# A third expert's first layer in seven half products, and two experts interleaved on four PSUM banks

## The chip, the cores and the metric

The kernel runs on one core of a Trainium2 chip. The metric is the device time of one execution in microseconds (us), the median of several runs. Engines are named as in the profile: PE is TensorE's matmul stream, PEld its weight loads, DVE is VectorE, ACT is ScalarE, POOL is GpSimd, SP is SyncE, which here only issues DMAs.

## What is computed

A windowed and causal attention over 4 batches, 8 heads and 768 positions gives a matrix x of 3072 tokens by 512 features. A dense mixture of four experts follows, in which every token goes through every expert:

```python
p = domain_probs / (domain_probs.sum(-1, keepdims=True) + 1e-09)
out = np.zeros((N, D), dtype=np.float32)          # N = 3072, D = 512
for e in range(E):                                # E = 4, F = 1024
    h = np.maximum(x @ w1[e], 0.0)
    out += p[:, e:e + 1] * (h @ w2[e])
```

The change touches only the product `x @ w1[e]` (the first layer) of the last tokens.

## The kernel before, in words

The order of every engine's instructions is written by hand: the kernel is one Python program that issues instructions in the order in which each engine will run them. Operands in SBUF are float16, sums in PSUM are float32. PSUM has eight banks here: four called pA, two called pV (attention's value products), two called pO.

The 24 tiles of 128 tokens are done as follows: three tiles and then one tile by plain matmuls (`plain_steps`), and then ten pairs of tiles, 256 tokens each (`pair_steps`, L1171), the pairs beginning at tiles 4, 6, ... 22. Attention for later tokens is mixed in between these steps; its last matmul in the trace is at 288.5 us, so that the last three pairs (tiles 18, 20 and 22) have the engines to themselves.

A pair has two layers.

**Layer 1** is `x @ w1[e]` for each expert, with the tokens already scaled by the expert's probability (`scale_inputs`, L1124, one DVE multiply of 128x1024 numbers, or two of 128x512 where the pair straddles a chunk of 384 tokens). A plain expert (`plain_layer1`, L1173) is four steps of eight matmuls of 256 columns, each step ended by one ACT relu that writes hidden values to the tile hA. An expert "by seven half products" (`winograd_layer1`, L1201) is Winograd's form of Strassen's scheme: the 512x1024 weights and the 512x256 tokens are cut into 2x2 blocks, and seven products of blocks take the place of eight. Each product is eight matmuls of 128 columns. The steps of one such expert are:

1. product on bank x, then an ACT copy of x to SBUF (`keep`, L1218)
2. product on a pA bank z, then a DVE add with saturation at zero (`add`, L1225) that writes one quarter of the hidden values
3. product added onto bank x, then a second ACT copy
4. product on bank y, a third ACT copy, and a small DVE subtraction on the tokens
5. product added onto x, then a DVE add
6. product added onto y, then a DVE add
7. product added onto x, then an ACT relu (L1258)

A product that adds onto a bank has to wait until the copy or add that reads that bank is done. Sums of token blocks (`scaled_sums`, L1147, three small DVE instructions) and sums of weight blocks (`first_weight_sums`, L1006, four DVE instructions of 128x1024, done once for an expert) feed the products. Before the last three pairs one expert (number 3) goes by half products; in the last three pairs experts 3 and 2 do (`EW`), and experts 0 and 1 are plain. Expert 3 has bank x = the first of the two pO banks taken for the pair and y = the second; expert 2 has them the other way round (L1265).

The order of steps in the last three pairs is the list at L1290, where a is expert 3, b expert 2, n the plain experts 0 and then 1. After each group of steps an extra operation may follow:

```python
((a, a, n), None), ((a, a, n), load_probs), ((a, a, n), None), ((n,), scaled_sums(EW[1])),
((a, b, n), None), ((b, b, n), first_sum(0)), ((b, b, n), first_sum(EW[0])),
((b, n, b), (first_sum(1), first_sum(EW[1])))
```

**Layer 2** (from L1307) is again seven products, of 16 matmuls of 256 columns each, over the hidden values of all four experts. It takes two new pO tiles, x and y. Its first product goes to x (L1363), its second to y, its seventh to x, read by the ACT copy at L1418. Beside it DVE makes the next pair's scaled tokens: expert 1 (L1370), expert 3, expert 0, the token sums of expert 3 and, as the last of them, expert 2 (L1394).

The weights of experts 0 and 1 lie in SBUF with pairs of columns interleaved (`w1_tile`, L344), so that a weight load of these reads with a step of two.

Of the kernel before, what the change touches and what calls it, by code (L numbers as in the profile page):

```python
# [11 lines left out]
FP32 = mybir.dt.float32  # L12
FP16 = mybir.dt.float16
AF = mybir.ActivationFunctionType
ALU = mybir.AluOpType
# [4 lines left out]
def kernel(  # L20
# [34 lines left out]
    P = 128  # L55
    B, H, S, D = q.shape
    E, DM, F = moe_w1.shape
# [5 lines left out]
    DMP = DM // P  # L63
# [19 lines left out]
    WT = 7  # L83
# [259 lines left out]

    def w1_tile(e, ct, ft):  # L344

        x = w1sb[:, e * DMP + ct, :]
        if in_pairs(e):
            x = x[:, ft // 2 * 2 * P : (ft // 2 + 1) * 2 * P]
            return x.rearrange("p (x j) -> p j x", j=2)[:, ft % 2, :]
        return x[:, ft * P : (ft + 1) * P]  # L350
# [202 lines left out]
    def mm_ns(cols):  # L553
        return cols / 2.4 + 2.5
# [434 lines left out]
    def minus(out, a, b):  # L989
        nc.vector.tensor_tensor(out=out, in0=a, in1=b, op=ALU.subtract)  # L990
# [15 lines left out]
    def first_weight_sums(e):  # L1006

        return [
            lambda: minus(t1[e, 0], w1_part(e, 0, 1), w1_part(e, 0, 0)),
            lambda: minus(t1[e, 1], w1_part(e, 1, 1), t1[e, 0]),  # L1010
            lambda: minus(t1[e, 2], w1_part(e, 1, 0), t1[e, 1]),
            lambda: minus(w1_part(e, 0, 1), w1_part(e, 1, 1), w1_part(e, 0, 1)),
        ]

    def room_for_more_sums():
# [6 lines left out]
        x = att.tile([P, DMP * PC], FP16, name="xs1", tag="q16", bufs=1)  # L1022
        own_room[EW[1]] = x.rearrange("p (c x) -> p c x", c=DMP)

    own_room = {}

    def last_weight_sum(e):
# [68 lines left out]
    PC = PT * P  # L1096
# [42 lines left out]
    def x_part(e, i, j):  # L1139
        return scaled(e)[:, j * KH : (j + 1) * KH, i * P : (i + 1) * P]  # L1140

    def x_sum(n):

        n0 = WT * NSH * P + n * KH * P
        return kSf[:, n0 : n0 + KH * P].rearrange("p (c x) -> p c x", c=KH)

    def scaled_sums(e):  # L1147

        nc.vector.tensor_tensor(
            out=x_sum(0), in0=x_part(e, 1, 0), in1=x_part(e, 1, 1), op=ALU.add  # L1150
        )
        minus(x_sum(1), x_sum(0), x_part(e, 0, 0))
        minus(x_part(e, 1, 0), x_part(e, 0, 0), x_part(e, 1, 0))

    def first_sum(e, n=1):
# [11 lines left out]

    def two(nt0):
        return nt0 >= pairs[-LAST]

    def pair_steps(nt0, nxt):  # L1171

        def plain_layer1(e):  # L1173
            xs = scaled(e)
            for f0 in range(0, FTP, 2):
                ps = bank()
                for f in range(2):
                    for ct in range(DMP):
                        nc.tensor.matmul(  # L1179
                            out=ps[:, f * PC : (f + 1) * PC],  # L1180
                            lhsT=w1_tile(e, ct, f0 + f),
                            rhs=xs[:, ct, :],
                            start=(ct == 0),
                            stop=(ct == DMP - 1),
                        )
                b0 = 2 * (f0 // HT)
                k0 = e * HT + f0 % HT
                nc.scalar.activation(  # L1188
                    out=blocks[:, b0 : b0 + 2, k0 : k0 + 2, :].rearrange(
                        "p t f x -> p f t x"  # L1190
                    ),
                    in_=ps.rearrange("p (f t x) -> p f t x", f=2, t=2),
                    func=AF.Relu,
                )
                yield 2 * DMP * mm_ns(PC), 0.5
# [2 lines left out]
        kept = [s1[:, (n % 2) * HT * P : (n % 2 + 1) * HT * P] for n in range(3)]  # L1198
        banks = [pO.tile([P, DM], FP32, name="pO", bufs=2) for _ in range(2)]

        def winograd_layer1(e, x, y):  # L1201

            ns = HT * KH * mm_ns(P)

            def product(ps, w, a, first):
                for f in range(HT):
                    for ct in range(KH):
                        nc.tensor.matmul(  # L1208
                            out=ps[:, f * P : (f + 1) * P],
                            lhsT=w[:, ct, f * P : (f + 1) * P],  # L1210
                            rhs=a[:, ct, :],
                            start=(first and f == 0 and ct == 0),
                            stop=(ct == KH - 1),
                            skip_group_check=True,
                        )

            def keep(n, ps):
                nc.scalar.copy(out=kept[n], in_=ps)  # L1218

            def block(n):  # L1220
                return blocks[:, n, e * HT : (e + 1) * HT, :]

            def add(n, ps, b):

                nc.vector._custom_dve(  # L1225
                    TENSOR_ADD_SAT,
                    out=block(b),
                    in0=ps.rearrange("p (f x) -> p f x", f=HT),
                    in1=kept[n].rearrange("p (f x) -> p f x", f=HT),
                    s0=LARGEST,  # L1230
                    s1=0.0,
                )

            def t(n):
                return t1[e, n]

            product(x, w1_part(e, 0, 0), x_part(e, 0, 0), True)
            keep(0, x)
            yield ns, 0.5
            z = bank()  # L1240
            product(z, w1_part(e, 1, 0), x_part(e, 0, 1), True)
            add(0, z, 0)
            yield ns, 0.5
            product(x, t(1), x_sum(1), False)
            keep(1, x)
            yield ns, 0.5
            product(y, t(0), x_sum(0), True)
            keep(2, y)
            minus(x_part(e, 0, 1), x_part(e, 0, 1), x_sum(1))
            yield ns, 0.5  # L1250
            product(x, w1_part(e, 0, 1), x_part(e, 1, 0), False)
            add(2, x, 3)
            yield ns, 0.5
            product(y, w1_part(e, 1, 1), x_part(e, 0, 1), False)
            add(1, y, 2)
            yield ns, 0.5
            product(x, t(2), x_part(e, 1, 1), False)
            nc.scalar.activation(  # L1258
                out=block(1), in_=x.rearrange("p (f x) -> p f x", f=HT), func=AF.Relu
            )  # L1260
            yield ns, 0.5

        a, b = (winograd_layer1(e, *y) for e, y in zip(EW, (banks, banks[::-1])))  # L1265

        more, last_more = [], None
        if nt0 == pairs[-LAST - 2]:
            room_for_more_sums()
            more = first_weight_sums(EW[1])  # L1270
        elif nt0 == pairs[-LAST - 1]:
            last_more = first_weight_sums(EW[1])[3]
        if not two(nt0):
            n = itertools.chain(*(plain_layer1(e) for e in range(E - 1)))
            order = (
                ((n,), lambda: scale_inputs(nt0, 1)),
                ((n,), more[0] if more else None),
                ((n, a), lambda: last_weight_sum(E - 1) if nt0 == pair0 else None),
                ((n, a), None),
                ((n, a), lambda: scale_inputs(nt0, 2)),  # L1280
                ((n, a), lambda: load_probs(nxt)),
                ((n, a), more[1] if more else None),
                ((n, a), more[2] if more else None),
                ((n, a), lambda: first_sum(0, 2)),
                ((n,), None),
                ((n, n), lambda: first_sum(2, 2)),
                ((), lambda: scale_inputs(nxt, 1) if two(nxt) else None),
            )
        else:
            n = itertools.chain(plain_layer1(0), plain_layer1(1))  # L1290
            order = (
                ((a, a, n), None),
                ((a, a, n), lambda: load_probs(nxt) if nxt else None),
                ((a, a, n), None),
                ((n,), lambda: scaled_sums(EW[1])),
                ((a, b, n), None),
                ((b, b, n), lambda: first_sum(0)),
                ((b, b, n), lambda: first_sum(EW[0])),
                ((b, n, b), lambda: (first_sum(1), first_sum(EW[1]))),
            )  # L1300
# [12 lines left out]
        def product(ps, a, b, first, middle=None):  # L1313
            for k in range(KT):
                nc.tensor.matmul(  # L1315
                    out=ps,
                    lhsT=a[:, k, :],
                    rhs=b(k),
                    start=(first and k == 0),
                    stop=(k == KT - 1),  # L1320
                    skip_group_check=not first,
                )
                if k == KT // 2 - 1:
                    if middle is not None:
                        middle()
                    yield KT // 2 * mm_ns(HN), PSHARE
# [4 lines left out]
        def t(n):  # L1331
            return lambda kt: tsb[:, n, kt, :]
# [26 lines left out]

        last = nxt is None  # L1360
        ahead = nxt and two(nxt)
        half = KT // 2 * mm_ns(HN), PSHARE
        yield from product(x, A11, b(0, 0), True)  # L1363
        keep(0, x)
# [207 lines left out]
```

## Time and profile before

| | |
|---|---|
| median of 6 runs | 377.98 us (377.49 to 378.89) |
| profiled execution | 377.49 us, span of instructions 375.7 us |
| PE busy in the span | 368.2 us (98%) |
| DVE / ACT / POOL busy | 271.4 / 228.0 / 112.5 us |
| mean granted TensorE clock | 0.998 |
| pair 20, layer 1 and layer 2 on PE | 321.32 to 334.56 and 334.56 to 346.78 us |
| pair 22, layer 1 | 346.78 to 360.02 us |

In the profile each row of a timeline is a run of like instructions: start, time until the last one ended, engine and line, operation, what it writes and reads, the count, and, where the engine stood idle before it, for how long and who ended that. Matmuls are pipelined, so the duration of a row of matmuls has the last one's latency in it; the pace of PE is read from the distance between starts.

### The profile page before, as it was taken

To read this page: it belongs to the slowest core of one execution; us is meant where nothing else is said; L and a number is where in the kernel's file an instruction comes from. 1 tells how busy PE (TensorE), PEld (TensorE's weight loads), DVE (VectorE), ACT (ScalarE), POOL (GpSimd) and SP (SyncE) were. 2 spreads that over 40 slices of the span, in tenths; PEclk is the share of its full clock that TensorE was granted. 3 is DMA by queue.
4 is the path that set the end of the run, shared out by engine and by line. 5 is a ranking of instruction groups with operands and counts; after the bars stand their busy time and mean duration, and the time that the engine had idled before them with its cause. 6 is when DMAs were issued, how large, how long until landed. Compare 5 with 4: busy or idle time off the path is not lost.

```text
span 375.7 us, 10100 instructions
## 1 busy us (share of the span) xinstructions
PE 368.2 (98%) x4128; PEld 310.9 (83%) x4128; DVE 271.4 (72%) x581; ACT 228.0 (61%) x475; POOL 112.5 (30%) x155
## 2 busy tenths in 40 slices
PE   8899999999999999999999999999999999999996
PEld 4754466668998988999989898998899998999995
DVE  7774868697787669868668858967768758559461
ACT  3863479547785785765776855784777361551630
POOL 8924673854057039115501650320000000000000
PEclk9999999999999999999999999999999999999999
DMA  9999999999599499978905991951220300300001
GB/s 167 151 202 208 194 185 193 172 177 145 97 116 156 87 98 128 161 106 70 192 5 66 172 154 27 130 117 11 72 68 3 114 2 0 114 2 23 36 2 57
DMA packets 123747, 39.24 MB, mean 104 GB/s; under 512 B 113728, under 2 KB 116356, under 8 KB 123700
## 3 DMA queue, kind: packets, MB, share of 16 engines
q0 software_dynamic: 85824, 19.01, 60.5%
q1 hardware_dynamic: 36276, 19.18, 22.4%
q8 instruction: 32, 0.52, 0.6%
q10 hardware_dynamic: 1600, 0.39, 0.5%
q14 instruction: 15, 0.12, 0.1%
HBM read 44.89 MB, written 6.34 MB: 136 GB/s over the span
## 4 chain that ended last, share of the span: by engine, by line
PE 95%; DVE 2%; ACT 2%; issue 0%; ACTq 0%
PE pO L1315 31%; PE pA L1179 25%; PE pO L1208 9%; PE pA L1050 7%; PE pO L1071 7%; PE pA L676 5%; PE pV L732 2%; PE pV L804 2%; PE pA L1208 2%; PE pO L446 1%; PE pA L574 1%; ACT es L694 1%; DVE xs L1135 1%; PE pA L1405 0%; ACT rc L822 0%; DVE xT L827 0%
## 5 line engine op out<-in xcount | busy, mean ns | idle before, releaser
L1315 PEld LDWEIGHTS <-hA 128*128 128x128 f16 x1104 | 104.8, 98 | 12.3
L1179 PE MATMUL pA<-xs,w1sb 128*128 128x256 f16 x864 | 109.3, 272 | 0.0
L1179 PEld LDWEIGHTS <-w1sb 128*128 128x128 f16 x864 | 80.7, 98 | 8.5
L1188 ACT ACTIVATE hA<-pA 128x512 f16<-128x512 f32 x108 | 64.4, 598 | 35.2 <-PE pA L1179 32.9
L1315 PE MATMUL pO<-w2sb,hA 128*128 128x256 f16 x640 | 76.7, 272 | 0.0
L694 ACT ACTIVATE es<-pA 128x384 f16<-128x384 f32 (+2 forms) x122 | 59.2, 511 | 26.6 <-PE pA L676 22.9
L306 POOL DMA_DIRECT2D vS<-in_v_dram x30 | 29.6, 986 | 110.0 <-PE pV L804 108.2
L1315 PE MATMUL pO<-tsb,hA 128*128 128x256 f16 x464 | 56.7, 272 | 0.0
L1135 DVE TENSOR_TENSOR xs<-xT,pB 128x1024 f16<-128x1024 f16 (+1 forms) x52 | 49.5, 970 | 1.3 <-DMA xT<-x_pair 1.2
L990 DVE TENSOR_TENSOR hA<-hA 128x1024 f16<-128x1024 f16 x60 | 39.6, 684 | 0.4
L1063 ACT ACTIVATE hA<-pA 128x384 f16<-128x384 f32 (+1 forms) x64 | 22.2, 385 | 19.5 <-PE pA L1050 19.3
L1050 PE MATMUL pA<-xT,w1sb 128*128 128x384 f16 (+1 forms) x256 | 31.1, 273 | 0.7 <-DMA w1sb<-in_moe_w_dram 0.3
L1071 PE MATMUL pO<-w2sb,hA 128*128 128x512 f16 x128 | 30.7, 379 | 0.0
L1335 ACT COPY s<-pO 128x256 f32<-128x256 f32 x31 | 11.6, 373 | 27.7 <-PE pO L1315 21.9
L827 DVE TENSOR_TENSOR xT<-pV,rc 64x384 f16<-64x384 f32 x37 | 20.5, 555 | 10.5 <-ACT rc L832 8.1
L1050 PEld LDWEIGHTS <-w1sb 128*128 128x128 f16 x256 | 19.4, 98 | 9.8 <-issue 1.5
L1208 PEld LDWEIGHTS <-w1sb 128*128 128x128 f16 x416 | 26.3, 98 | 1.1 <-issue 0.2
L1225 DVE CUSTOM_DVE_ANT_0 hA<-pO,s 128x512 f16<-128x512 f32 x26 | 17.7, 689 | 12.5 <-PE pO L1208 8.8
L822 ACT ACTIVATE rc<-pV,eps 64x384 f32<-64x384 f32 x37 | 21.3, 576 | 6.5 <-PE pV L804 5.9
L698 DVE TENSOR_TENSOR es<-es,mS 128x384 f16<-128x384 f16 (+1 forms) x40 | 13.7, 344 | 15.0 <-ACT es L694 15.0
L676 PE MATMUL pA<-qT,kR 128*128 128x384 f16 (+2 forms) x120 | 22.9, 278 | 0.6 <-DVE kR L593 0.6
L1218 ACT COPY s<-pO 128x512 f32<-128x512 f32 x39 | 22.5, 586 | 1.4 <-PE pO L1208 1.2
(144 smaller groups left out, 486.6 us busy)
## 6 DMA issues: line engine op xcount, KB each, us to landing
pB<-p_rows SPq DMA_DIRECT2D x10, 512.0 KB
out_dram<-o SPq DMA_DIRECT2D x19, 256.0 KB
w1sb<-in_moe_w_dram POOLq DMA_DIRECT2D x8, 512.0 KB, 9.1
w2sb<-in_moe_w_dram POOLq DMA_DIRECT2D x4, 1024.0 KB, 12.2
vS<-in_v_dram POOLq DMA_DIRECT2D x30, 112.0 KB, 4.3
k_rows<-in_k_dram POOLq DMA_DIRECT2D x18, 128.0 KB, 5.2
q<-in_q_dram POOLq DMA_DIRECT2D x18, 128.0 KB, 6.9
vR<-in_v_dram POOLq DMA_DIRECT2D x24, 48.0 KB, 5.6
```

The costliest lines, as they stand in the source:

```text
L306: gp.dma_start(out=t[:, :, own_v(h)], in_=windows_of(v, b, h, c))
L676: nc.tensor.matmul(out=ps[:, o : o + nq], lhsT=key_tile(b, c, h, t), rhs=qTs[b, c][:, hp, q0 : q0 + nq], start=(n == 0 or not first), stop ...
L694: nc.scalar.activation(out=es[:, 0:cols], in_=ps[:, 0:cols], func=AF.Exp, scale=SC)
L990: nc.vector.tensor_tensor(out=out, in0=a, in1=b, op=ALU.subtract)
L1050: nc.tensor.matmul(out=pss[ft][:, 0:cols_n], lhsT=w1_tile(e, ct, ft), rhs=x[:, ct, :], start=(n == 0), stop=(n == DMP - 1),)
L1071: nc.tensor.matmul(out=ps_o, lhsT=hs[:, ft, j * P : (j + 1) * P], rhs=w2sb[:, e * FTP + ft, :], start=(ft == 0), stop=(ft == FTP - 1),)
L1135: nc.vector.tensor_tensor(out=o, in0=xin, in1=pb.to_broadcast([P, DMP, n, P]), op=ALU.mult)
L1179: nc.tensor.matmul(out=ps[:, f * PC : (f + 1) * PC], lhsT=w1_tile(e, ct, f0 + f), rhs=xs[:, ct, :], start=(ct == 0), stop=(ct == DMP - 1),)
L1188: nc.scalar.activation(out=blocks[:, b0 : b0 + 2, k0 : k0 + 2, :].rearrange("p t f x -> p f t x"), in_=ps.rearrange("p (f t x) -> p f t x" ...
L1208: nc.tensor.matmul(out=ps[:, f * P : (f + 1) * P], lhsT=w[:, ct, f * P : (f + 1) * P], rhs=a[:, ct, :], start=(first and f == 0 and ct == ...
L1218: nc.scalar.copy(out=kept[n], in_=ps)
L1315: nc.tensor.matmul(out=ps, lhsT=a[:, k, :], rhs=b(k), start=(first and k == 0), stop=(k == KT - 1), skip_group_check=not first,)
```

## The change

In the last two pairs (tiles 20 and 22) expert 1 too goes by seven half products (`third`), and expert 0 alone stays plain. There expert 3 and expert 2 run step by step in turn, a, b, a, b; expert 2 has two banks of its own (pV) and its kept copies lie in the tile kSf, whose attention keys are no longer needed. Expert 1 follows on the pO banks. Its sums of weights and its scaled tokens lie in vSf, also free by then. The weight sums for it are made in pair 18: three between layer 1's steps, the fourth at that pair's end.

```diff
+    def w_tile(e, x, ft):
...
+    EW3 = E - 3
+    def room_for_third():
+        n = KH * FN
+        for i in range(3):
+            t1[EW3, i] = vSf[:, i * n : (i + 1) * n].rearrange("p (c f) -> p c f", c=KH)
+    def inputs_for_third():
+        n0 = 3 * KH * FN
+        x = vSf[:, n0 : n0 + DMP * PC]
+        own_room[EW3] = x.rearrange("p (c x) -> p c x", c=DMP)
...
+    second_set = set()
+    def x_sum(e, n):
+        n0 = (2 * P * 8 if e in second_set else WT * NSH * P) + n * KH * P
...
+    def three(nt0):
+        return nt0 >= pairs[-2]
...
-                            lhsT=w[:, ct, f * P : (f + 1) * P],
+                            lhsT=w_tile(e, w[:, ct, :], f),
...
         a, b = (winograd_layer1(e, *y) for e, y in zip(EW, (banks, banks[::-1])))
+        if three(nt0):
+            second_set.add(EW[1])
+            more_kept = kSf[:, 0 : 4 * HT * P].bitcast(FP32)
+            more_kept = [more_kept[:, n * HT * P : (n + 1) * HT * P] for n in (0, 1, 0)]
+            more_banks = [pV.tile([P, DM], FP32, name="pV", bufs=2) for _ in range(2)]
+            b = winograd_layer1(EW[1], *more_banks, more_kept)
+            third = winograd_layer1(EW3, *banks)
...
+        elif nt0 == pairs[-3]:
+            room_for_third()
+            more = first_weight_sums(EW3)
+            last_more = more[3]
...
+        elif three(nt0):
+            n = plain_layer1(0)
+            order = (
+                ((), lambda: scaled_sums(EW[1])),
+                ((a, b, a, b), lambda: load_probs(nxt) if nxt else None),
+                ((a, b, a, b), None),
+                ((a, b, a, b), None),
+                ((a, b), lambda: scaled_sums(EW3)),
+                ((n,), None),
+                ((third, third, n), lambda: first_sum(EW[0])),
+                ((third, third, n), lambda: first_sum(EW[1])),
+                ((third, third, n), lambda: first_sum(0)),
+                ((third,), lambda: first_sum(EW3)),
+            )
         else:
...
-                ((a, a, n), None),
+                ((a, a, n), more[0] if more else None),
                 ((a, a, n), lambda: load_probs(nxt) if nxt else None),
-                ((a, a, n), None),
+                ((a, a, n), more[1] if more else None),
                 ((n,), lambda: scaled_sums(EW[1])),
-                ((a, b, n), None),
+                ((a, b, n), more[2] if more else None),
...
+        if ahead and three(nxt):
+            inputs_for_third()
```

More of the change, by code (lines that the diff above doesn't have):

```diff
@@ L344, in w1_tile @@
     def w1_tile(e, ct, ft):
-        x = w1sb[:, e * DMP + ct, :]
+        return w_tile(e, w1sb[:, e * DMP + ct, :], ft)
+    def w_tile(e, x, ft):
         if in_pairs(e):
@@ L1140, in x_part @@
         return scaled(e)[:, j * KH : (j + 1) * KH, i * P : (i + 1) * P]
-    def x_sum(n):
-        n0 = WT * NSH * P + n * KH * P
+    second_set = set()
+    def x_sum(e, n):
+        n0 = (2 * P * 8 if e in second_set else WT * NSH * P) + n * KH * P
         return kSf[:, n0 : n0 + KH * P].rearrange("p (c x) -> p c x", c=KH)
@@ L1149, in scaled_sums @@
         nc.vector.tensor_tensor(
-            out=x_sum(0), in0=x_part(e, 1, 0), in1=x_part(e, 1, 1), op=ALU.add
+            out=x_sum(e, 0), in0=x_part(e, 1, 0), in1=x_part(e, 1, 1), op=ALU.add
         )
-        minus(x_sum(1), x_sum(0), x_part(e, 0, 0))
+        minus(x_sum(e, 1), x_sum(e, 0), x_part(e, 0, 0))
         minus(x_part(e, 1, 0), x_part(e, 0, 0), x_part(e, 1, 0))
@@ L1199, in pair_steps, with winograd_layer1 @@
         banks = [pO.tile([P, DM], FP32, name="pO", bufs=2) for _ in range(2)]
-        def winograd_layer1(e, x, y):
+        def winograd_layer1(e, x, y, kept=kept):
             ns = HT * KH * mm_ns(P)
@@ L1243, in winograd_layer1 @@
             yield ns, 0.5
-            product(x, t(1), x_sum(1), False)
+            product(x, t(1), x_sum(e, 1), False)
             keep(1, x)
             yield ns, 0.5
-            product(y, t(0), x_sum(0), True)
+            product(y, t(0), x_sum(e, 0), True)
             keep(2, y)
-            minus(x_part(e, 0, 1), x_part(e, 0, 1), x_sum(1))
+            minus(x_part(e, 0, 1), x_part(e, 0, 1), x_sum(e, 1))
             yield ns, 0.5
```

## The prediction

> **What bounds the kernel now.** I read the page first, then the stages of the last pairs, then the timelines of PE, DVE and ACT there.
>
> ```profile
> PE 368.2 (98%) x4128; PEld 310.9 (83%) x4128; DVE 271.4 (72%) x581; ACT 228.0 (61%) x475; POOL 112.5 (30%) x155
> ...
> PE 95%; DVE 2%; ACT 2%; issue 0%; ACTq 0%
> ```
>
> PE is busy 98% of the span and carries 95% of the chain that ended last. The stages show that this holds where the change works. The columns are PE, PEld, DVE, ACT and POOL busy, the clock, and the DMA's share and rate:
>
> ```profile
> 321.32:334.56 13.24, 13.24 (x179) 12.51 (x177) 6.47 (x15) 8.39 (x16) 0.00 (x0) 1.00 0.24 81
> 334.56:346.78 12.22, 12.22 (x115) 10.96 (x113) 10.42 (x18) 1.95 (x5) 0.00 (x0) 1.00 0.01 1
> 346.78:360.02 13.24, 13.24 (x178) 12.51 (x176) 6.34 (x14) 8.38 (x16) 0.00 (x0) 1.00 0.11 41
> ```
>
> Layer 1 of pairs 20 and 22 is 13.24 us of PE without a gap, at full clock. DVE has about 6.8 us idle in it, ACT 4.9, POOL is empty. So a change in PE's work there is worth its whole length, unless PE comes to wait for DVE or ACT. The pace of PE comes from the starts in its timeline:
>
> ```profile
> 346.78 0.61 PE L1208 MATMUL pO<-xs,w1sb 128*128 128x128 f16 x8
> 347.23 0.61 PE L1208 MATMUL pA<-xs,w1sb 128*128 128x128 f16 x8
> 347.68 1.04 PE L1179 MATMUL pA<-xs,w1sb 128*128 128x256 f16 x8
> 348.55 1.06 PE L1208 MATMUL pO<-kS,t1sb 128*128 128x128 f16 x16
> 349.44 1.04 PE L1179 MATMUL pA<-xs,w1sb 128*128 128x256 f16 x8
> ```
>
> A half product (eight matmuls of 128 columns) takes 0.447 us (0.89 for sixteen), a plain step (eight of 256) 0.873. Check: 14 x 0.447 + 8 x 0.873 = 13.24, which is layer 1.
>
> **The work on PE.** In each of pairs 20 and 22 the change takes away four plain steps (expert 1), 4 x 0.873 = 3.49 us, and adds seven half products, 7 x 0.447 = 3.13. That saves 0.366 us a pair, 0.73 us in all. Layer 1 becomes 21 x 0.447 + 4 x 0.873 = 12.88 us. No cheaper pace is in sight, so 0.73 is the most that PE can give.
>
> [...] First, expert 1's weights are read with a step of two columns, so far only under 256-column matmuls in the pairs. But the single tile did plain 128-column matmuls with both layouts:
>
> ```profile
> 76.81 1.95 PE L1050 MATMUL pA<-xT,w1sb 128*128 128x128 f16 x32
> 78.59 1.89 PE L1071 MATMUL pO<-w2sb,hA 128*128 128x512 f16 x8
> 80.32 1.95 PE L1050 MATMUL pA<-xT,w1sb 128*128 128x128 f16 x32
> 82.11 1.89 PE L1071 MATMUL pO<-w2sb,hA 128*128 128x512 f16 x8
> ```
>
> Expert 1 (step of two) took 1.78 us for 32, expert 2 (no step) 1.79. The step costs nothing. [...] The rows here, each matmul with its own load, give 447 / 8 = 56 ns. [...]
>
> **What PE may have to wait for.** ACT's count stays: four relus go, three copies and a relu come, of 0.59 to 0.60 us each. DVE gains per pair three adds (0.60 apart when queued), three token sums (0.81) and a small subtraction (0.28), 2.9 us in 6.8 us of idle time. So neither engine becomes the bound; only moments can. The lags: ACT starts 0.24 us after a product's last issue, DVE 0.30. PE starts 0.06 after a DVE result (a cast from 14.27 for 0.54 us let PE go at 14.87). I use 0.06 for ACT's results too.
>
> In the turn a, b, a, b a bank is needed again after three other half products, 1.34 us. A copy takes 0.24 + 0.59 + 0.06 = 0.89. Two DVE adds in a row are the tightest: b's add starts 0.30 + 0.60 - 0.447 = 0.45 us after its product, and 0.45 + 0.69 + 0.06 = 1.20. Cover 0.14 us. If that cover is gone, each 0.1 us of DVE delay costs PE 0.1 us, once a pair. In the expert that comes last, plain steps lie between and the cover is 0.27 or more.
>
> The start of layer 2 is closer. Expert 1 runs on the pO banks, its first bank x ends with a relu just ahead of layer 2, its y with an add that is one plain step and one half product older. Which one does layer 2's first product get? The trace tells how banks are handed out. Each pair takes two pO tiles, then two more, so by plain rotation the next pair's first product would lie in the bank of the seventh product of layer 2. Yet at 346.78 it starts, while the copy that reads the seventh product runs only then:
>
> ```profile
> 346.98 0.37 ACT L1418 COPY o<-pO 128x256 f32<-128x256 f32 x1 [4.87 <-PE pO L1315]
> ```
>
> So the bank whose last reader comes earlier in the program is taken first. By this rule layer 2 begins on expert 1's y. Its add is behind another: 0.46 + 0.69 + 0.06 = 1.21 us after the product, and PE comes after 0.873 + 0.447 = 1.32. Cover 0.11, no wait. The first sums that layer 2 needs then end some 1.3 us into it, as now, where its third product starts at 3.49.
>
> The one wait that I do expect is at the second half product. Expert 2 now starts 0.447 us into layer 1 instead of 6.2, and its scaled tokens are the last thing that DVE makes in layer 2:
>
> ```profile
> 345.76 0.42 DVE L1338 TENSOR_TENSOR o<-pO,s 128x256 f32<-128x256 f32 x1
> 346.10 1.21 DVE L1135 TENSOR_TENSOR xs<-xT,pB 128x1024 f16<-128x1024 f16 x1
> 348.09 0.69 DVE L1225 CUSTOM_DVE_ANT_0 hA<-pA,s 128x512 f16<-128x512 f32 x1 [0.78 <-ACT s L1218]
> ```
>
> In pair 22 they are there at 347.31 + 0.06 = 347.37, and PE wants them at 347.23: 0.14 us of waiting, with all later matmuls queued behind. In pair 20 they come in two pieces (320.70, for 1.28 us), one for each tile, and the half products up to b's second read only the first, done at 321.34, ahead of 321.77. If PE must wait for both, until 322.04, that is another 0.27 us. I take 0, since the two pieces are two instructions on separate columns, and keep 0.27 for the range. It can't be a gain: PE starts nothing earlier than it does now. Expert 2's token sums, now at once after that scaling, end about 1.9 us (pair 20, behind the fourth weight sum) and 1.1 us into layer 1; its third half product comes at 2.2.
>
> **Edits at nothing.** Pair 18 gets three weight sums of 0.68 us in layer 1, where DVE idles 1.80, 2.39 and 1.10 us. The first delays expert 3's token subtraction from 298.05 to 298.65, and PE needs it at 299.8. The fourth, 0.6 us at the pair's end, delays DVE's first add to about 1.9 us into layer 1, and the bank behind it is not needed before 3.6. If these covers failed, each would cost at most its own 0.6. The probability load is one SP issue of 0.37 us; it already waits in SP's queue until the last scaling has read the old block, and is needed some 12 us later. POOL has nothing. The new places, kSf and vSf, were last read by attention at 288.5, before pair 18. Copies from the pV banks are priced like those from pO (0.59), as those from pA are (0.60).
>
> **Sum.** -0.73 + 0.14 = -0.59 us on the profiled execution: 377.49 to 376.9. The median stands 0.49 above that execution, so 377.98 - 0.59 = 377.4 us.
>
> **Rivals.**
>
> - *Slower: layer 2's first product gets the bank of expert 1's seventh.* Then PE waits for the relu: 0.24, some 0.05 behind the last plain relu, 0.59 and 0.06, so 0.94 us a pair. 377.4 + 1.88 = 379.3. For it: expert 1 has its banks in the order opposite to b's now, and its relu is the last thing ahead of layer 2. Against it: the early start at 346.78. It decides once the bank is that of the relu, and costs nothing otherwise.
> - *DVE late at the two thin covers* (0.14 and 0.11 us). DVE's queue is fuller, adds wait on two engines. 0.1 to 0.4 us a pair: 377.6 to 378.2. For it: two covers below 0.15. Against it: spacings in the trace repeat to 0.02 us.
> - *No wait at all*, the second half product's included: 377.98 - 0.73 = 377.25.
> [...]
>
> **How the numbers follow.** As reckoned 0.68, DVE late 0.15, no wait 0.10, the wrong bank 0.06, the loads 0.01. The range 376.95 to 378.4 takes in the first three, with the 0.27 us of pair 20 and a few tenths by which medians of such runs move; it leaves out the last two. About 0.2%, 0.76 us, is what a measurement can tell from no change, and PE can give no more than 0.73. So faster by more than that needs scatter besides: 0.22. Within 0.2%: 0.66. Slower: the wrong bank, the loads and a tail of DVE late, 0.12.
>
> **What would show it.** In the profile after: 21 half products and 4 plain steps in about 12.9 us in pairs 20 and 22; a PE gap near 0.14 us ahead of the second half product in pair 22 and none in pair 20; no gap ahead of layer 2; DVE 2.9 us busier in each layer 1; pair 18 at 13.24 and 12.23 us as before. [...] A change elsewhere in the span, in the first 295 us, would be outside all this.

## The result and the profile after

The changed kernel takes 376.77 us (median of 16 runs, 376.28 to 377.99) against 377.79 us for the kernel before (36 runs beside it). The ratio is 0.9973, with a 95% interval of 0.9965 to 0.9981: it is faster by 1.02 us, between 0.7 and 1.3. The forecast was 377.4, a gain of 0.59. The sign was right, the size was not, and the time lies just below the forecast range. Of the 0.6 us between forecast and time, 0.19 is the starting point (the kernel before has a median of 377.79 in these 36 runs, 377.98 in the six of the forecast), and 0.43 is gain that was not forecast.

The page of the changed kernel shows that PE is still the bound:

```profile
PE 367.0 (98%) x4176; PEld 310.3 (83%) x4176; DVE 279.3 (75%) x599; ACT 227.5 (61%) x475; POOL 112.2 (30%) x155
...
PE 94%; DVE 2%; ACT 2%; DMA 1%; issue 0%; ACTq 0%
```

PE has 48 more matmuls and is busy 1.2 us less. The stages are layer 1 of pair 20, its layer 2, and layer 1 of pair 22 (columns as before: PE, PEld, DVE, ACT and POOL busy, clock, DMA share and rate):

```profile
321.30:334.17 12.87, 12.87 (x203) 12.51 (x200) 9.57 (x23) 8.08 (x16) 0.00 (x0) 1.00 0.25 83
334.17:346.39 12.22, 12.22 (x115) 10.96 (x113) 10.42 (x18) 1.96 (x5) 0.00 (x0) 1.00 0.01 1
346.39:359.40 13.01, 13.01 (x202) 12.55 (x200) 9.03 (x21) 8.13 (x16) 0.00 (x0) 1.00 0.12 42
```

Layer 1 went from 13.24 to 12.87 us in pair 20 and to 13.01 in pair 22. Forecast: 12.88, and 12.88 + 0.14 = 13.02. Layer 2 and pair 18 are as they were. PE's timeline at the start of pair 22 has the one wait that was forecast:

```profile
346.39 0.61 PE L1228 MATMUL pO<-xs,w1sb 128*128 128x128 f16 x8
346.98 0.61 PE L1228 MATMUL pV<-xs,w1sb 128*128 128x128 f16 x8
347.42 1.06 PE L1228 MATMUL pA<-xs,w1sb 128*128 128x128 f16 x16
```

The second half product starts 0.59 us after the first instead of 0.447, while in DVE's timeline the scaling for it runs until 346.93:

```profile
345.38 0.42 DVE L1384 TENSOR_TENSOR o<-pO,s 128x256 f32<-128x256 f32 x1
345.71 1.22 DVE L1150 TENSOR_TENSOR xs<-xT,pB 128x1024 f16<-128x1024 f16 x1
```

So PE accounts for what was forecast: from the first half product of pair 18 to the start of the last matmul it takes 76.38 us before and 75.78 after, 0.60 less. The other 0.42 us lie behind the last matmul. From its start to the end of the span the kernel before takes 3.52 us, the changed one 3.10. These are the last two sums on DVE and the issues of the last two stores on SP, first before:

```profile
372.04 0.29 DVE L1412 TENSOR_TENSOR o<-pA,s 128x128 f32<-128x128 f32 x1 [0.91 <-PE pA L1405]
372.49 0.29 DVE L1412 TENSOR_TENSOR o<-pA,s 128x128 f32<-128x128 f32 x1 [0.16 <-PE pA L1405]
...
372.35 1.20 SPq L1415 DMA_DIRECT2D out_dram<-o  x2
```

then after:

```profile
371.05 0.29 DVE L1460 TENSOR_TENSOR o<-pA,s 128x128 f32<-128x128 f32 x1 [0.54 <-PE pA L1453]
371.87 0.29 DVE L1460 TENSOR_TENSOR o<-pA,s 128x128 f32<-128x128 f32 x1 [0.53 <-PE pA L1453]
...
371.39 1.13 SPq L1463 DMA_DIRECT2D out_dram<-o  x2
```

The last product of layer 2 is done in two halves of 16 matmuls, each with its sum and its store. After, the two sums start 0.82 us apart, nearly as far as the halves of the product (0.89); before, 0.45 us, because the first one is late. The wait of the first sum is a row of its own on DVE, an EVENT_SEMAPHORE. The rows of that wait and of the stores, by their lines, first before and then after:

```profile
L1412 DVEq EVENT_SEMAPHORE  x1: 21/21/21, 371.6 to 371.6; - x1
L1415 SPq DMA_DIRECT2D out_dram<-o x2: 332/535/738, 372.4 to 372.8; - x2
...
L1460 DVEq EVENT_SEMAPHORE  x1: 21/21/21, 371.0 to 371.0; - x1
L1463 SPq DMA_DIRECT2D out_dram<-o x2: 333/390/448, 371.4 to 372.2; - x2
```

The columns after the count are the shortest, median and longest duration in ns and the first and last start in us. In the kernel before the wait ended at 371.62 and the sum started at 372.04: for 0.41 us DVE had its input and did nothing. In the changed kernel the same step takes 0.05 us. The second sum starts 0.26 us after the last matmul in both kernels, so the late first sum does not delay it. It pushes the first store back, so that the two stores are issued 0.46 us apart instead of 0.79, and the issue of the second takes 0.74 us on SP instead of 0.33. That is 0.41 of the 0.42 us.

**Two theories.** Theory C: what makes DVE stand still is the place of the instruction in DVE's stream. Counting DVE's rows in the trace from 1, those of waits included, the late sum is number 704 before and number 727 after (the expectation of experiment 1 says "counted from 0"; the trace has 703 rows ahead of it). The page of before lists two DMA queues of kind instruction, q8 with 32 packets (0.52 MB) and q14 with 15 (0.12 MB). The last packet of q14, of 8192 bytes, starts at 372.81, when DVE was near its 705th row; two others of the 15 start when it is at row 192 (99.72) and at row 320 (161.81), 128 rows apart. The profile doesn't name the engine that a packet is for; that one of them brings a block of 128 instructions of DVE is the author's estimate from these rows. If a new block begins with number 704, DVE pays for it with its input ready, at the one place of the kernel where nothing hides it. The change adds 23 rows to DVE's stream, so that another instruction stands at the boundary. Theory S: the end scatters from run to run, and the half products or the alternation on four banks gain more than the trace of one execution shows.

### The profile page after: what moved, and what is told of

It is laid out like the page before. It is cut to its first block, busy times and chain, and to the rows that moved or that the text cites. A ratio compares the mean times of both kernels' runs of the same rounds, so it can differ in the third digit from the quotient of the medians.

```text
span 374.7 us, 10225 instructions
## 1 busy us (share of the span) xinstructions
PE 367.0 (98%) x4176; PEld 310.3 (83%) x4176; DVE 279.3 (75%) x599; ACT 227.5 (61%) x475; POOL 112.2 (30%) x155
## 4 chain that ended last, share of the span: by engine, by line
PE 94%; DVE 2%; ACT 2%; DMA 1%; issue 0%; ACTq 0%
PE pO L1361 31%; PE pA L1199 23%; PE pO L1228 9%; PE pA L1065 7%; PE pO L1086 7%; PE pA L678 5%; PE pV L734 2%; PE pV L806 2%; PE pA L1228 2%; PE pV L1228 1%; DMA hA<-in_q_dram 1%; ACT es L696 1%; PE pA L576 1%; DVE xs L1150 1%; PE pA L1453 0%; ACT rc L824 0%
## 5 line engine op out<-in xcount | busy, mean ns | idle before, releaser
L1199 PE MATMUL pA<-xs,w1sb 128*128 128x256 f16 x800 | 101.3, 273 | 0.0
L1199 PEld LDWEIGHTS <-w1sb 128*128 128x128 f16 x800 | 74.7, 98 | 7.9
L1208 ACT ACTIVATE hA<-pA 128x512 f16<-128x512 f32 x100 | 59.6, 598 | 31.2 <-PE pA L1199 29.0
L1150 DVE TENSOR_TENSOR xs<-xT,pB 128x1024 f16<-128x1024 f16 (+1 forms) x49 | 46.9, 976 | 1.4 <-DMA xT<-x_pair 1.4
L1228 PEld LDWEIGHTS <-w1sb 128*128 128x128 f16 x480 | 29.6, 98 | 1.1 <-issue 0.2
L1065 PEld LDWEIGHTS <-w1sb 128*128 128x128 f16 x256 | 19.3, 98 | 9.8 <-issue 1.4
```

The costliest lines, as they stand in the source:

```text
L1065: nc.tensor.matmul(out=pss[ft][:, 0:cols_n], lhsT=w1_tile(e, ct, ft), rhs=x[:, ct, :], start=(n == 0), stop=(n == DMP - 1),)
L1150: nc.vector.tensor_tensor(out=o, in0=xin, in1=pb.to_broadcast([P, DMP, n, P]), op=ALU.mult)
L1199: nc.tensor.matmul(out=ps[:, f * PC : (f + 1) * PC], lhsT=w1_tile(e, ct, f0 + f), rhs=xs[:, ct, :], start=(ct == 0), stop=(ct == DMP - 1),)
L1208: nc.scalar.activation(out=blocks[:, b0 : b0 + 2, k0 : k0 + 2, :].rearrange("p t f x -> p f t x"), in_=ps.rearrange("p (f t x) -> p f t x" ...
L1228: nc.tensor.matmul(out=ps[:, f * P : (f + 1) * P], lhsT=w_tile(e, w[:, ct, :], f), rhs=a[:, ct, :], start=(first and f == 0 and ct == 0), ...
```

## The experiments

In the table, the third column runs from the first half product of pair 18 to the start of the last matmul, the fourth from there to the end of the span. Both are read in each kernel's trace. The ratio is to the kernel before in the same series.

| kernel | ratio, 95% interval | PE, us | end, us |
|---|---|---|---|
| before | 1 | 76.38 | 3.52 |
| changed | 0.9973 (0.9965 to 0.9981) | 75.78 | 3.10 |
| 1 before again | 1.0002 (0.9993 to 1.0011) | 76.38 | 3.50 |
| 2 before, one DVE row more | 0.9990 (0.9983 to 0.9998) | 76.38 | 3.10 |
| 3 before, eight DVE rows more | 0.9985 (0.9979 to 0.9991) | 76.38 | 3.11 |
| 4 other order of scaling | 0.9980 (0.9971 to 0.9989) | 75.65 | 3.10 |
| 5 changed, boundary put back | 1.0053 (1.0040 to 1.0066) | 75.78 | 3.46 |
| 6 alternation only | 0.9993 (0.9984 to 1.0002) | 76.51 | 3.10 |
| 7 change in one pair | 0.9968 (0.9956 to 0.9980) | 76.15 | 3.11 |
| 8 other order of new tiles | 0.9981 (0.9971 to 0.9992) | 75.78 | 3.11 |
| 9 changed again | 0.9980 (0.9966 to 0.9995) | 75.78 | 3.10 |
| 10 as 4, again | 0.9978 (0.9968 to 0.9989) | 75.65 | 3.10 |
| 11 layer 2 on the relu's bank | 1.0024 (1.0018 to 1.0031) | 77.55 | 3.10 |
| 12 two banks | 1.0110 (1.0094 to 1.0125) | 81.22 | 3.10 |

The PE column repeats to 0.01 us, while the part ahead of pair 18 ends anywhere from 295.75 to 297.23 us in traces that share its instructions. So the time alone can't tell differences of 0.1 to 0.2 us apart, and the two columns can.

**1. The kernel before, again.** No edit.

> The kernel before, unchanged, as a control. Both theories: no difference beyond 0.1 us. Theory C (the 0.41 us beyond PE's saving come from the end of the program: VectorE's instruction number 704, counted from 0, is the first of the last two sums, and the instruction stream is fetched in blocks, so that VectorE stands still there for some 0.35 us with its input ready): the profile shows again a hole of about 0.41 us between the wait and the first of the last two sums, and the last store's issue takes about 0.7 us. Theory S (scatter of the tail from run to run): the hole is gone or elsewhere in this second profile.

The late sum is back: 0.39 us from the end of its wait to its start, the second store's issue takes 0.72 us, the end 3.50 us. Theory S would have had it move.

**2 and 3. One and eight instructions more on DVE.**

```diff
+    idle = pers.tile([P, 1], FP32, name="idle")
...
+        for _ in range(1 if nt0 == pairs[-2] else 0):    # 8 in experiment 3
+            nc.vector.memset(idle[0:1, :], 0.0)
```

> The kernel before with one memset of a single unused number on VectorE, at the start of pair 20, so that every later VectorE instruction moves by one place. Theory C: the block boundary now falls in front of the wait instead of behind it, where VectorE idles anyway for TensorE; the first of the last two sums starts 0.05 us after its wait, and the time falls by about 0.4 us, to 0.9989 of before. Theory S, or a gain that comes from the half products alone: no difference (0.06 us of a free engine).

> The kernel before with eight such memsets. Theory C: the boundary falls among VectorE's instructions of layer 2 of the last pair, some 8 us earlier, where it has slack; about 0.4 us less than before, as with one. Theory S: no difference, or a loss of up to 0.5 us of VectorE time in layer 1 of pair 20, which is covered.

One memset that no one reads makes the kernel 0.38 us faster (0.08 to 0.64), eight 0.57 (0.34 to 0.79). The one-row kernel's last two sums:

```profile
373.04 0.29 DVE L1416 TENSOR_TENSOR o<-pA,s 128x128 f32<-128x128 f32 x1 [0.54 <-PE pA L1409]
373.87 0.29 DVE L1416 TENSOR_TENSOR o<-pA,s 128x128 f32<-128x128 f32 x1 [0.53 <-PE pA L1409]
```

They are 0.83 us apart, and the end takes 3.10 us, as in the changed kernel. PE's column is untouched. Theory C expected this, theory S nothing.

**5. The boundary put back.** The changed kernel with 105 memsets, after which the sum is number 832 = 704 + 128.

```diff
+    idle = pers.tile([P, 1], FP32, name="idle")
...
+        for _ in range(15 if nt0 < pairs[-3] else 0):
+            nc.vector.memset(idle[0:1, :], 0.0)
```

> The changed kernel with 105 memsets of a single unused number on VectorE, 15 in each of the seven pairs 4 to 16, so that the first of the last two sums is again the first instruction of a block of 128 (place 832 = 704 + 128). Theory C: the hole of 0.35 to 0.41 us is back in front of it, and the time rises from 1.02 below before to about 0.6 below, the saving that was predicted on TensorE. Theory S: as the changed kernel. Both: the memsets themselves, some 0.06 us each, 0.9 us a pair, lie in VectorE's idle time unless the timeline of TensorE shows otherwise.

The pause is back where theory C puts it, and with it the end of 3.46 us:

```profile
374.73 0.29 DVE L1464 TENSOR_TENSOR o<-pA,s 128x128 f32<-128x128 f32 x1 [0.89 <-PE pA L1457]
375.20 0.29 DVE L1464 TENSOR_TENSOR o<-pA,s 128x128 f32<-128x128 f32 x1 [0.18 <-PE pA L1457]
```

The time itself rose far more than expected, to 379.95 us: the memsets were not hidden. Pair 18 began at 299.16 us instead of 295.83, and the waits of PE name DVE's scaling:

```profile
PE pA L1203 <- DVE xs L1151: 2.2, 4, 0.8
```

These waits are 2.2 of the 3.3 us. Placed at the start of a pair, the memsets stood ahead of the scaling that the pair's plain steps need. So only the end of this run is evidence, not its time.

**4 and 10. The wait that was left.** In layer 2 of pairs 18 and 20 expert 2's tokens are scaled ahead of expert 0's.

```diff
-            scale_inputs(nxt, 0)
+            scale_inputs(nxt, EW[1] if ahead and three(nxt) else 0)
...
-            scale_inputs(nxt, EW[1] if ahead else EW[0])
+            if ahead and three(nxt):
+                scale_inputs(nxt, 0)
+            else:
+                scale_inputs(nxt, EW[1] if ahead else EW[0])
```

> The changed kernel with expert 2's tokens scaled ahead of expert 0's in layer 2 of pairs 18 and 20. If the 0.145 us gap in front of the second half product of pair 22 is the wait for that scaling, it goes, nothing takes its place (expert 0's tokens are read first 6.2 us into layer 1), and the kernel is 0.14 us faster than the changed one: 1.16 us below before, ratio 0.9969. If the gap is something else that belongs to the first use of the two new banks, it stays.

> The changed kernel with expert 2's tokens scaled ahead of expert 0's, once more, now beside the changed kernel itself. On TensorE 0.13 us less from the start of pair 18 to the last matmul, as the first trace of it showed (75.65 against 75.78); in time 0.13 below the changed kernel, which five rounds may not tell from it.

PE's timeline of experiment 4 at the start of pair 22:

```profile
346.49 0.61 PE L1228 MATMUL pO<-xs,w1sb 128*128 128x128 f16 x8
346.93 0.61 PE L1228 MATMUL pV<-xs,w1sb 128*128 128x128 f16 x8
347.38 0.83 PE L1228 MATMUL pA<-xs,w1sb 128*128 128x128 f16 x12
```

The second half product follows after 0.44 us; the wait is gone, and PE's column is 75.65 twice, 0.13 below the changed kernel. The times (0.9980 and 0.9978, the changed kernel 0.9980 beside the second) can't tell it from the changed kernel; the first is less of a gain than the expected 0.9969, which lies just outside its interval. By the traces it is the fastest of these kernels.

**6. The alternation alone.** Expert 1 stays plain, experts 3 and 2 alternate on four banks.

```diff
-            third = winograd_layer1(EW3, *banks)
...
+            n = itertools.chain(plain_layer1(0), plain_layer1(1))
...
+                ((a, b), None),
+                ((n, n), lambda: first_sum(EW[0])),
+                ((n, n), lambda: first_sum(EW[1])),
+                ((n, n), lambda: first_sum(0)),
+                ((n, n), lambda: first_sum(1)),
```

> The changed kernel with expert 1 plain in the last two pairs: experts 3 and 2 still alternate on four banks, then eight plain steps follow. If the saving on TensorE is that of the half products alone, layer 1 of pair 20 takes 13.24 us as before and that of pair 22 takes 13.38 (the wait of 0.14 for the scaled tokens). In time: 0.14 above before, less 0.4 if theory C is right, since VectorE's instructions have moved by two places, so 0.27 below; by theory S 0.14 above. If the alternation itself saves something, layer 1 is shorter than 13.24.

PE's column is 76.51, 0.13 above before: the alternation saves nothing by itself and brings the wait. The end is 3.10, as theory C expects with the sum at number 706. In time it is not told from before (0.9984 to 1.0002).

**7. One pair.** `three` holds for the last pair alone, the weight sums move to pair 20.

```diff
-        return nt0 >= pairs[-2]
+        return nt0 >= pairs[-1]
...
-        elif nt0 == pairs[-3]:
+        elif nt0 == pairs[-2]:
```

> The changed kernel with expert 1 by half products and the alternation in the last pair alone, the weight sums one pair later. Layer 1 of pair 20 is 13.24 us as before, that of pair 22 12.88 and the wait of 0.14. So 0.22 us below before on TensorE; with theory C 0.63 below, with theory S 0.22.

76.15 is 0.23 below before, 0.37 above the changed kernel: half products in one pair are worth 0.37 us, less 0.14 for the wait. The time, 0.9968 from five runs, is 0.8 to 1.7 us below before. That is more than the 0.63 expected and than the 0.64 that the two columns make; where the rest comes from is not shown.

**8 and 11. Layer 2 on the bank of the relu.** The rival's price. Experiment 8 took the two new tiles in the other order, 11 reuses the two tiles of layer 1.

```diff
+        x, y = (pO.tile([P, DM], FP32, name="pO", bufs=2)[:, 0:HN] for _ in range(2))   # 8
+        if three(nt0):
+            x, y = y, x
```

```diff
+        x, y = banks if three(nt0) else (                                              # 11
+            pO.tile([P, DM], FP32, name="pO", bufs=2) for _ in range(2)
+        )
+        x, y = x[:, 0:HN], y[:, 0:HN]
```

> The changed kernel with the two output banks of layer 2 taken in the other order in the last two pairs, so that layer 2's first product must wait for the relu of expert 1's seventh half product. The rival of the prediction put this at 0.94 us a pair: gaps of that size ahead of layer 2 in pairs 20 and 22, and 1.88 us more than the changed kernel, 0.86 above before. If layer 2 began on that bank already, nothing changes or the time falls.

> The changed kernel with layer 2 of the last two pairs on the very two tiles of layer 1, its first product on the bank of expert 1's seventh half product. (Taking two new tiles in the other order changed nothing: the slots are given at the first use, so the program came out the same.) The rival of the prediction prices this at 0.94 us a pair: two gaps of about 0.94 us ahead of layer 2, 1.88 us more than the changed kernel.

Experiment 8 changed nothing, 75.78 us on PE as in the changed kernel. The author's reading is that a tile gets its slot when it is first used; so it is one more run of the changed kernel. Experiment 11 has the wait, here at the start of layer 2 in pair 20, the relu first:

```profile
334.33 0.59 ACT L1278 ACTIVATE hA<-pO 128x512 f16<-128x512 f32 x1
334.47 0.92 DVE L1174 TENSOR_TENSOR hA<-hA 128x512 f16<-128x512 f16 x2 [0.56 <-ACT hA L1208]
334.98 2.23 PE L1363 MATMUL pO<-w2sb,hA 128*128 128x256 f16 x19 [0.73 <-ACT hA L1278]
```

PE starts 0.06 us after the relu's end. Both pairs together cost 1.77 us on PE against 1.88 expected, so the rival was priced nearly rightly. It did not happen because layer 2 begins on the other bank. In the changed kernel its first product starts ahead of the relu, and 0.18 us after the add that reads the other bank:

```profile
332.70 1.29 DVE L1245 CUSTOM_DVE_ANT_0 hA<-pO,s 128x512 f16<-128x512 f32 x2 [1.40 <-PE pO L1228]
334.17 3.66 PE L1361 MATMUL pO<-w2sb,hA 128*128 128x256 f16 x32
334.42 0.59 ACT L1278 ACTIVATE hA<-pO 128x512 f16<-128x512 f32 x1
```

**12. Two banks.** Expert 1 by half products, but the three experts one after the other on two banks.

```diff
-            b = winograd_layer1(EW[1], *more_banks, more_kept)
...
+                ((a, a, n), lambda: load_probs(nxt) if nxt else None),
+                ((a, a, n), None),
+                ((a, a, n), None),
+                ((a, b, b), lambda: scaled_sums(EW3)),
+                ((b, b, n), lambda: first_sum(EW[0])),
+                ((b, b, b), lambda: first_sum(0)),
+                ((third, third, third, third), lambda: first_sum(EW[1])),
+                ((third, third, third), lambda: first_sum(EW3)),
```

> The changed kernel without the alternation: expert 1 still by half products in the last two pairs, but experts 3, 2 and 1 one after the other on the two pO banks, with the four plain steps between. If the four banks are what hides the copies and adds, TensorE waits wherever only one other half product lies between two on one bank: 0.89 - 0.45 = 0.44 us behind a copy and 1.05 - 0.45 = 0.60 behind an add, about two of the first for expert 2, two of the first and one of the second for expert 1 and one ahead of layer 2, in all 2.0 to 2.7 us a pair, 4 to 5.4 us in time. If the banks don't matter, the time stays at that of the changed kernel.

PE's column is 81.22, 2.72 us a pair above the changed kernel, just above the 2.0 to 2.7 that were expected. The longest waits of PE in layer 1 name the adds and the copies (us in total, times, longest):

```profile
PE pO L1228 <- DVE hA L1245: 1.7, 4, 0.4
PE pO L1228 <- ACT s L1238: 1.6, 6, 0.3
```

The run changes the banks and the order of steps together. So the alternation on four banks gains nothing by itself, but with one plain expert left to fill the gaps the half products would lose without it.

## Why the prediction was right and wrong

**Right, the work on PE.** 0.366 us a pair was forecast. Layer 1 of pair 20 went from 13.24 to 12.87; experiments 6 and 7 give 0.36 and 0.37 for one pair (76.51 - 76.15 and 76.15 - 75.78).

**Right, the pace of the half products.** 56 ns for each 128-column matmul with its own weight load was taken from the rows. In layer 1 of pair 20 the half products still start 0.445 us apart, 56 ns a matmul. Expert 1's step of two columns cost nothing: its half products start 0.45 us apart too (328.42 and 328.87). The chance of 0.01 for "the loads" was the author's estimate for half products further apart than that; no run shows such a term, and the two traces show 0.447 us before and 0.445 after.

**Right, the waits.** 0.14 us at the second half product of pair 22, none in pair 20, none ahead of layer 2 and none at the two thin covers of 0.14 and 0.11 us. Experiment 4 shows that the wait was for the order of the scalings. Ahead of layer 2 the cover is 0.18 - 0.06 = 0.12 us in the trace, against 0.11 reckoned. Experiments 11 and 12 show what the banks are worth: the wrong bank costs 0.89 us a pair, two banks instead of four 2.72.

**Wrong, the sum.** The step that failed is "-0.73 + 0.14 = -0.59 us on the profiled execution". It has only PE's terms and takes what lies behind the last matmul for the same length. That part was 0.42 us shorter, because the change put 23 more rows into DVE's stream and thereby moved a pause away from the first of the last two sums. Nothing in that part is edited by the diff, and the prediction says nothing of it: the row of that sum, at 372.04 with 0.91 us idle, stands in the trace of before, as does the distance of 0.45 us to the second where PE's halves are 0.89 apart. With the term the sum is -0.60 - 0.42 = -1.02, against 1.02 measured; from 377.79 the forecast -0.59 would have given 377.2. By experiments 1, 2 and 5 this gain belongs to the place of an instruction and not to the half products: experiment 2 has it without the change, and experiment 5 loses it with the change. That the change brought it is luck.

**What stays open.** Shown is that the first of the last two sums starts late when it is at place 704 (before and its repetition) or 832 (experiment 5), and in none of the other kernels, where it has another place. In the changed kernel place 704 is an add in layer 1 of pair 22. The row ahead of it there is a wait too, and DVE idles 0.22 us longer before it than before the like add of pair 20, while PE doesn't wait for it:

```profile
329.74 0.69 DVE L1245 CUSTOM_DVE_ANT_0 hA<-pA,s 128x512 f16<-128x512 f32 x1 [0.92 <-ACT s L1238]
355.20 0.69 DVE L1245 CUSTOM_DVE_ANT_0 hA<-pA,s 128x512 f16<-128x512 f32 x1 [1.14 <-ACT s L1238]
```

The place alone doesn't make the pause. In all these cases the row just ahead of the place is a wait. Where a working instruction stands ahead of place 704, the next one starts at most 0.06 us after its end (experiments 3, 5, 7 and 12; in experiment 6 it waits for PE). That suggests that reaching the place takes about 0.4 us, which a working instruction ahead hides, but no run was made for it. That the cause is the loading of a block of instructions is argued, not shown. For it: the 128 between the two places, and a packet of 8192 bytes that starts within 1.5 us of place 704 in every trace, at 355.85 us in the changed kernel and at 365.29 in experiment 3. Against the simplest form of it: in the kernel before that packet starts 0.77 us after the late sum, so the sum did not wait for this packet, and at rows 448 and 576 none starts within 1.8 us.

Open too is why the second store's issue took 0.70 to 0.74 us in before and in experiments 1 and 5. The short distance to the issue ahead, 0.46 to 0.47 us, is not enough: in the changed kernel the first of the two issues comes 0.475 us after an earlier store's and takes 0.45. In the three slow cases, and in no other trace, an instruction packet of 8192 bytes starts within 0.04 us of that issue. Nothing here tells the two apart.

## What to carry to other kernels

Where one engine is busy without a gap, the count of its instructions times their pace, read from distances between starts, gave the saving here to 0.01 us a pair, and each moved consumer has to be checked against the one producer that used to have slack. Read the end of the kernel like any other stage, from the last big instruction to the end of the span: if an engine there starts well after its wait was over (0.41 us here), its place in the instruction stream may be to blame, and one idle instruction ahead of it tells (experiment 2, an end of 3.10 us instead of 3.52). A gain that comes from such a place is not the change's own and can vanish with the next edit (experiment 5, 3.46 us again).

## What the runs showed of the hardware

A DVE instruction whose input was ready started 0.39 to 0.41 us after its wait had ended, in the three traces where its place in the stream was 704 or 832 (before, experiments 1 and 5); the same sum took 0.04 to 0.05 us in the eleven others. The packets that start within 1.5 us of these places have 8192 bytes. Whether the pause is the loading of instructions is not shown. The pause was not hidden in the tail: 0.35 to 0.37 us of DVE, and 0.36 to 0.42 us of the kernel, through the store that follows. Matmuls of 128 columns, each with its own weight load, started 56 ns apart in the kernels before and after (0.447 and 0.445 us for eight).
